# An order edge between each transfer of SyncE and ScalarE and the one written just before it

## The chip, the cores and the metric

The kernel runs on one core of one Trainium2 chip. The metric is the device time of one execution in microseconds (us); lower is better. The kernel before takes 667.28 us, the median of three runs (664.82 to 667.79). The engines are named as in the profile: PE (matmul), PEld (its weight loads), DVE (vector), ACT (scalar), POOL (GpSimd) and SP (sync). SP computes nothing: its queue only issues transfers. ACT both computes and issues transfers, and its queue is one list, in which a transfer that waits holds up the computation behind it.

## The reference

Two blocks run one after the other. The first is a delta-rule attention over 4 batches x 8 heads x 768 steps x 48 channels; the second is a feed-forward block on the 3072 tokens that come out of it.

```python
k_n = k / (np.linalg.norm(k, axis=-1, keepdims=True) + 1e-06)
for t in range(S):
    kt, vt, bt = (k_n[:, :, t], v[:, :, t], beta[:, :, t, None])
    y[:, :, t] = np.einsum('bhd,bhde->bhe', q[:, :, t], state)
    v_old = np.einsum('bhde,bhd->bhe', state, kt)
    state = state + bt[:, :, :, None] * np.einsum('bhd,bhe->bhde', kt, vt - v_old)
...
x = np.ascontiguousarray(attn_out.transpose(0, 2, 1, 3)).reshape(B * S, H * D)
h = x @ w_in            # 384 -> 2048
g = h * np.cos(h)
return (g @ w_out)      # 2048 -> 384
```

The two weight arrays come as 64-bit floats: the kernel loads them as pairs of 32-bit words and makes 32-bit floats of them itself.

## The kernel before

**Attention.** The 768 steps are cut into 24 units of 32 steps (`unit(n)`, n = 0 to 23), and two units make a pair m. For a unit, k, q and v are loaded (`load`, line 356; from unit 8 on q and k also as transposable blocks, `load_blocks`, line 375), a Gram matrix of the keys is made on PE (`gram`, line 611), scaled on DVE (line 622) and put into DRAM (`gram_put`, line 663). For each pair the Gram matrices are read back in another layout (`gram_get`, lines 676 and 684), and the triangular systems are inverted column by column (`invert`, lines 721 and 728): for the first pair on DVE, for the other eleven on POOL, which is the longest work of that engine. The inverse goes through DRAM (`put`, line 742) and comes back per unit as the tile `zt` (`get`, lines 753 and 761), which `solve` (line 851) needs. The state is carried from unit to unit on PE and DVE (`update`, line 876, `update_out`, line 884).

**Feed-forward.** Two units together give 256 tokens. Their hidden layer is made of products on PE, plain ones for the first two pairs of units (`hidden`, line 935), and a fast scheme with sums of blocks for the others (`layer`, line 1113, with copies of its banks on ACT, lines 1125 and 1127, and sums of x on POOL or DVE, line 1028). The gate h cos h goes through ACT, DVE, ACT, DVE (lines 976, 983, 992, 995), and the output layer through PE (lines 1136 and 1193), ACT or DVE (lines 1232 and 1245) and a store (line 1257). The weights come in 28 slices: `narrow_load` (line 473, tile `pairs`), `narrow_split` on ACT (lines 481 and 483), `narrow_shift` on DVE (lines 487 and 492), `narrow_add` on POOL (line 496).

**The order of the work** is written out by hand: `Order.LINE` is a list of all tasks, and `Order.run` emits them in this order. `Order.OTHER` says which transfers go on ACT's queue instead of SP's: 139 on ACT, 526 on SP. After the last task the loop at lines 1721 to 1725 gives every instruction an order edge to the one written before it on the same engine (`pin`, line 1697). Such an edge (`DependencyClass.NoSync`) is drawn when the program is built: it holds a place in the order, and it is no semaphore wait.

**What the build adds.** The build interleaves the five lists of instructions, hands out buffers of a pool as it goes, and gives every transfer of SP and ACT one of eight counters (DMAHW0 to DMAHW7) in turn, in the order in which it has placed the transfers of both queues. A transfer is issued only once the transfer before it on its counter has landed. In the built program nearly every transfer carries such a wait, for the transfer eight places earlier in that order, whichever queue that one is on. In this text this is the transfer's *predecessor*.

**Buffers.** The pool tag `g` has eight buffers (`GATES = 8`). The gate tiles `g_ffn`, the weight slices `pairs` and some small tiles take them in turn; whoever gets a buffer waits for the last user of that buffer.

Of the kernel before, what the change touches and what calls it, by code (L numbers as in the profile page):

```python
# [218 lines left out]
def kernel(  # L219
# [1477 lines left out]
    def pin(ins, on):  # L1697
        tc.add_manual_dep(
            ins,
            on.name,  # L1700
            mybir.DependencyInfo(
                mybir.DependencyClass.NoSync, mybir.DependencyReason.DATA
            ),
            reason="order",
        )
# [12 lines left out]
    order.run(wrote)  # L1718


    last = {}
    for ins in nc.cur_bb.bb.instructions:
        if ins.engine in last:
            pin(ins, last[ins.engine])
        last[ins.engine] = ins


# [29 lines left out]
```

## Time and profile before

| what | value |
|---|---|
| median of three runs | 667.28 us |
| lowest and highest | 664.82 and 667.79 us |
| span of the profiled execution | 663.5 us |
| PE busy | 595.1 us (90%) |
| POOL busy | 484.3 us (73%) |
| DVE busy | 504.2 us (76%) |
| ACT busy | 294.7 us (44%) |
| transfers on SP's queue (q1) | 160372 packets, 32.31 MB, 26.4% of 16 engines |
| transfers on ACT's queue (q10) | 54896 packets, 17.28 MB, 12.1% of 16 engines |
| mean granted TensorE clock | 0.952 |

The span runs from the first to the last instruction of one profiled execution. The profile gives no time of its own beside that span; the three timed runs lie 1.3 to 4.3 us above it. The profile's views are these: busy times by engine; 40 slices of the span; the chain of work that ended last; groups of instructions by line; waits, with who waited for whom; and the timeline of an engine. A row such as `ACT g_ffn L1125 <- DMA gb<-g_dr: 11.4, 1, 11.4` reads: the instruction of line 1125 on ACT started after 11.4 us of idle time, once, and what ended the wait was the landing of a transfer that writes `gb`.

### The profile page before, as it was taken

How to read it: one execution, taken by the hardware profiler on the slowest of the kernel's cores; microseconds unless marked ns; L12 is line 12 of the kernel's file. 1: busy time of each engine (PE TensorE's matmuls, PEld its weight loads, DVE VectorE, ACT ScalarE, POOL GpSimd, SP SyncE). 2: the span in 40 equal slices, each digit the busy share in tenths (PEclk: the TensorE clock that was granted, in tenths of full speed). 3: DMA queues.
4: the chain of work that ended last, by engine and by line, in shares of the span. 5: the costliest groups of instructions: out<-in, count | busy, mean ns of one | idle time of the engine just before them, and what ended most of it. 6: DMA issues, size and time to landing. Idle time of an engine off the chain costs nothing.

```text
span 663.5 us, 23460 instructions
## 1 busy us (share of the span) xinstructions
PE 595.1 (90%) x9784; PEld 559.0 (84%) x9784; DVE 504.2 (76%) x996; ACT 294.7 (44%) x518; POOL 484.3 (73%) x852
## 2 busy tenths in 40 slices
PE   3315799889999999999999999999789999999997
PEld 3304698677898999989999999999789999999996
DVE  5775588689799887868888888898758678667581
ACT  3424475454234544545545436444235453546340
POOL 4447888868898898888898988988666688413322
PEclk9855599989999999999999999999989999999999
DMA  8786764762164352344451462542311400200000
GB/s 173 166 185 155 180 139 120 156 133 43 44 113 62 64 94 43 74 85 71 67 100 27 80 98 41 95 78 52 73 24 33 92 10 26 34 2 26 1 24 25
DMA packets 215629, 51.52 MB, mean 78 GB/s; under 512 B 207076, under 2 KB 210420, under 8 KB 215524
## 3 DMA queue, kind: packets, MB, share of 16 engines
q1 hardware_dynamic: 160372, 32.31, 26.4%
q10 hardware_dynamic: 54896, 17.28, 12.1%
q8 instruction: 77, 1.26, 0.8%
q0 software_dynamic: 256, 0.45, 0.3%
q14 instruction: 28, 0.23, 0.1%
HBM read 39.24 MB, written 10.75 MB: 75 GB/s over the span
## 4 chain that ended last, share of the span: by engine, by line
PE 61%; POOL 19%; DMA 7%; DVE 4%; issue 4%; SPq 2%; ACT 1%; ACTq 0%; POOLq 0%; DVEq 0%
PE p_h L1113 20%; PE p_out L1193 20%; POOL z L728 8%; POOL part L721 7%; PE p_h L935 6%; PE p_out L1136 3%; DMA vp<-in_v_dram 3%; PE p_kq L781 2%; POOL x_sum L1028 2%; PE p_s L876 2%; PE p_kq L893 2%; PE p_u L851 2%; PE p_o L1193 2%; DMA pairs<-in_moe_w_in_dram 1%; PE p_g L611 1%
## 5 line engine op out<-in xcount | busy, mean ns | idle before, releaser
L721 POOL TENSOR_TENSOR part<-z,gb 128x126 f32<-128x126 f32 (+22 forms) x341 | 151.9, 445 | 36.2 <-ACT z L700 8.2
L728 POOL TENSOR_TENSOR z<-z,part 128x126 f32<-128x126 f32 (+22 forms) x341 | 155.3, 455 | 26.7
L1193 PE MATMUL p_out<-w_out,g_ffn 128*128 128x192 f32 x672 | 120.0, 329 | 0.0
L1193 PEld LDWEIGHTS p_out<-w_out,g_ffn 128*128 128x128 f32 x672 | 108.0, 190 | 1.2
L1209 POOL TENSOR_TENSOR g_ffn<-g_ffn 128x512 f32<-128x512 f32 x43 | 57.8, 1349 | 56.6 <-PE p_out L1193 30.9
L1113 PE MATMUL p_h<-x_sum,w_in 128*128 128x128 f32 x640 | 83.2, 279 | 7.9 <-ACT g_ffn L1125 6.4
L1193 PE MATMUL p_out<-w_sum,g_ffn 128*128 128x192 f32 x496 | 88.9, 328 | 0.1
L992 ACT ACTIVATE turns<-turns,halfpi 128x512 f32<-128x512 f32 x96 | 68.3, 719 | 42.5 <-DVE turns L983 35.6
L1113 PEld LDWEIGHTS p_h<-x_sum,w_in 128*128 128x128 f32 x640 | 78.4, 193 | 9.2 <-ACT g_ffn L1125 6.7
L1193 PEld LDWEIGHTS p_out<-w_sum,g_ffn 128*128 128x128 f32 x496 | 79.6, 190 | 0.7 <-DVE o L1245 0.3
L976 ACT ACTIVATE turns<-g_ffn,quarter_turn 128x512 int32<-128x512 f32 x70 | 50.1, 720 | 48.8 <-DVE g_ffn L1130 25.7
L1130 DVE TENSOR_TENSOR g_ffn<-g_ffn,p_h 128x512 f32<-128x512 f32 x80 | 54.6, 683 | 17.0 <-PE p_h L1113 14.9
L906 ACT COPY y<-p_kq 32x384 f32<-32x384 f32 x96 | 45.1, 470 | 37.2 <-PE p_kq L893 31.9
L995 DVE TENSOR_TENSOR g_ffn<-turns,g_ffn 128x512 f32<-128x512 f32 x70 | 53.3, 770 | 8.9 <-ACT turns L992 8.8
L983 DVE SCALAR_TENSOR_TENSOR turns<-g_ffn,turns 128x512 f32<-128x512 f32 x70 | 56.5, 812 | 1.6 <-ACT turns L976 1.4
L1113 PE MATMUL p_h<-x_sum,in_sum 128*128 128x128 f32 x400 | 53.8, 279 | 0.1
L935 PE MATMUL p_h<-x_ffn,w_in 128*128 128x128 f32 x384 | 48.8, 288 | 5.5 <-DVE g_ffn L995 5.5
L935 PEld LDWEIGHTS p_h<-x_ffn,w_in 128*128 128x128 f32 x384 | 46.9, 202 | 6.6 <-DVE g_ffn L995 5.9
L1113 PEld LDWEIGHTS p_h<-x_sum,in_sum 128*128 128x128 f32 x400 | 50.0, 194 | 0.9 <-ACT g_ffn L1125 0.4
L1245 DVE SCALAR_TENSOR_TENSOR o<-p_out,o 128x192 f32<-128x192 f32 x74 | 25.2, 353 | 31.5 <-PE p_out L1193 30.6
L530 POOL TENSOR_TENSOR knrm<-ksum,halves 128x16 f32<-128x16 f32 (+1 forms) x14 | 38.9, 2777 | 11.1 <-DVE ksum L518 11.0
L1113 PE MATMUL p_h<-x_ffn,w_in 128*128 128x128 f32 x320 | 43.1, 279 | 0.0
(133 smaller groups left out, 1011.0 us busy)
## 6 DMA issues: line engine op xcount, KB each, us to landing
pairs<-in_moe_w_out_dram SPq DMA_DIRECT2D x12, 384.0 KB
vp<-in_v_dram SPq DMA_DIRECT2D x88, 48.0 KB
pairs<-in_moe_w_in_dram ACTq DMA_DIRECT2D x7, 512.0 KB
gb<-g_dr ACTq DMA_DIRECT2D x12, 256.0 KB
kp<-in_k_dram SPq DMA_DIRECT2D x128, 24.0 KB
out_dram<-o ACTq DMA_DIRECT2D x14, 192.0 KB
pairs<-in_moe_w_in_dram SPq DMA_DIRECT2D x5, 512.0 KB
gb<-g_dr SPq DMA_DIRECT2D x10, 256.0 KB
```

The source lines that it names most:

```text
L721: eng.tensor_tensor(out=part, in0=z[:, 0:rows, j, None].to_broadcast(shape), in1=a[:, j, None, j + 1 :].to_broadcast(shape), op=ALU.mult,)
L728: eng.tensor_tensor(out=behind, in0=behind, in1=part, op=ALU.subtract)
L906: nc.scalar.copy(by_parity(y[quarter(b)]), p_kq[quarter(b ^ 1), :, b % 2])
L935: nc.tensor.matmul(p_h[:, i], w_in[:, t, (4 * k + i) * 128 : (4 * k + i + 1) * 128], xts[p][:, t, unit * 128 : (unit + 1) * 128], start=(i ...
L976: nc.scalar.activation(turns[p, f], hidden_of(p, f), AF.Identity, bias=quarter_turn, scale=TURN)
L983: nc.vector.scalar_tensor_tensor(out=r, in0=hidden_of(p, f), scalar=TURN, in1=t, op0=ALU.mult, op1=ALU.subtract,)
L992: nc.scalar.activation(r, r, AF.Sin, bias=halfpi, scale=2.0 * math.pi)
L995: nc.vector.tensor_tensor(out=place(p, f), in0=step_of(rests.pop((p, f)), f), in1=step_of(hidden_of(p, f), f), op=ALU.mult,)
L1113: nc.tensor.matmul(p_h[:, e], in_block(*w)[:, e], x_of(p, b), start=new and e == 0, stop=True, skip_group_check=True,)
L1130: nc.vector.tensor_tensor(out=part_of(p, to), in0=part_of(p, one), in1=part_of(p, two), op=op)
L1193: nc.tensor.matmul(p_o, left(p, part, a)[:, e % 4], right(e, b), start=(e == 0), stop=(e == FT // 2 - 1), skip_group_check=True,)
L1209: either(("left", p, x, s), nc.vector, nc.gpsimd).tensor_tensor(out=left(p, s, to), in0=left(p, s, one), in1=left(p, s, two), op=op)
```

## The change

The loop that pins each engine's instructions also remembers the last transfer that is not POOL's. If the next such transfer stands on the other queue, it gets an order edge to the one written before it. With the edges along each engine, all 665 transfers of SP and ACT then stand in one fixed order, that of `Order.LINE`. The edges are of the same kind as those already there. No instruction is added or taken away.

```diff
-    last = {}
+    last, before = {}, None
     for ins in nc.cur_bb.bb.instructions:
         if ins.engine in last:
             pin(ins, last[ins.engine])
         last[ins.engine] = ins
+        if isinstance(ins, mybir.InstDMACopy) and ins.engine != mybir.EngineType.Pool:
+            if before is not None and before.engine != ins.engine:
+                pin(ins, before)
+            before = ins
```

## The prediction

> **What bounds the kernel.** I read the page first, then the stretches, then the waits and timelines of the stretches where PE is not full. The first rows are the page's.
>
> ```profile
> span 663.5 us, 23460 instructions
> PE   3315799889999999999999999999789999999997
> POOL 4447888868898898888898988988666688413322
> DMA  8786764762164352344451462542311400200000
> PE 61%; POOL 19%; DMA 7%; DVE 4%; issue 4%; SPq 2%; ACT 1%; ACTq 0%; POOLq 0%; DVEq 0%
> ```
>
> One slice is 16.6 us. Counted from 1, PE is nearly full but for the first five slices, a dent in slices 8 and 9 (116 to 149 us), and one in slices 29 and 30 (464 to 498 us). The transfer engines are busy only at the start. POOL is at 8 to 9 tenths from slice 10 to slice 28, so what is late on POOL stays late there. The busy times by stretch (columns: stretch, length, PE, PEld, DVE, ACT, POOL, granted clock, transfer engines' share, GB/s) say the same:
>
> ```profile
> 0.00:66.00 66.00, 23.09 (x648) 19.38 (x648) 43.07 (x119) 24.66 (x45) 35.73 (x51) 0.72 0.79 170
> 126.00:150.00 24.00, 17.88 (x150) 16.34 (x143) 16.28 (x29) 11.12 (x21) 17.74 (x32) 0.93 0.72 144
> 470.00:484.00 14.00, 7.59 (x54) 7.30 (x53) 6.38 (x13) 2.57 (x6) 5.71 (x13) 0.86 0.49 91
> 484.00:664.00 180.00, 174.70 (x2298) 169.62 (x2298) 120.68 (x221) 75.91 (x130) 92.51 (x161) 0.98 0.12 26
> ```
>
> Behind 484 us PE is busy for 174.7 of 180 us and DMA for 0.12: a shift there goes to the end whole. Three places are open to transfers: the start, 126 to 150 us, and 470 to 484 us.
>
> **What the change does.** I compared the wait lists of the two built programs. The order on every queue is the same in both, and no wait between the two queues is added as such; what the edges fix is the order in which the eight counters are dealt. 387 of 665 transfers get another predecessor. In the program before, eight transfers wait for one that is written *after* them; in the program after none does. One pair of `g` buffers is exchanged as well. No instruction is added, so there is no issue time to price. The price of each edit is the landing of its new predecessor against the time at which the transfer was issued in this trace.
>
> **470 to 484 us: a wait goes (-6.7).** The timeline of ACT, then of SP:
>
> ```profile
> 470.16 0.32 ACTq L375 DMA_DIRECT2D qp<-in_k_dram  x1
> 470.57 0.59 ACT L1125 COPY p_h<-p_h 128x512 f32<-128x512 f32 x1
> 481.14 1.41 ACTq L375 DMA_DIRECT2D qp<-in_k_dram  x3
> 482.59 1.07 ACT L1125 COPY g_ffn<-p_h 128x512 f32<-128x512 f32 x2 [11.43 <-DMA gb<-g_dr]
> ```
> ```profile
> 476.67 0.37 SPq L742 DMA_DIRECT2D z_dr<-z  x1
> 477.27 1.35 SPq L684 DMA_DIRECT2D gb<-g_dr  x2
> ```
>
> ACT issues one of four block loads at 470.16, and the second only at 481.14. The second's predecessor is SP's `gb` load of 477.27, written four places after it, which stands behind SP's put of `z`, which waits for POOL's inverse. So ACT waits 10.7 us (481.14 - 470.48) for a transfer that it has no use for, and the two copies behind (line 1125) keep PE's banks occupied. The waits of 470 to 485 us give PE's price:
>
> ```profile
> ACT g_ffn L1125 <- DMA gb<-g_dr: 11.4, 1, 11.4
> PEld p_h L1113 <- ACT g_ffn L1125: 6.7, 1, 6.7
> ```
>
> After the change the three loads' predecessors are Gram puts that SP issued at 459.3 to 460.4 and that landed by 462.4, so ACT passes at once. Its copies are then done at about 476, and PE, which now stops at 477.0 and resumes at 483.72, goes on without a stop. What is late next there is SP's four `zt` loads, landed by 483.3; `solve` reads them at 493.39. With the shift of +1.9 below they land at 485.2, and PE, 4.8 early, comes at 488.5: 3.4 us to spare. POOL's next column (484.84) waits for the `gb` load at 481-482 as before and has some 4 us to spare. So I take the whole 6.7.
>
> **0 to 66 us: waits come (+4.7).** Here 32 transfers have a new predecessor that landed after their issue in this trace, 17 on SP (15.0 us in sum) and 15 on ACT (20.1 us). The chain of waits shows where landings carry the end (start, us, what):
>
> ```profile
> 24.55 6.13 DMA vp<-in_v_dram
> ...
> 44.66 3.92 DMA vp<-in_v_dram
> ...
> 61.88 4.14 DMA pairs<-in_moe_w_in_dram
> 66.03 2.75 DMA kp<-in_k_dram
> ```
>
> Written order makes SP's Gram put of 27.94 wait for the v load of 24.55, which lands at 30.68, and with the +0.5 carried from before it comes 3.25 late. ACT's Gram put of 37.94 then waits for a v load of 33.57 that landed at 39.67, itself 1.7 late: +3.5. ACT's `halves_z` loads (46.4 to 48.6) wait for the v load landed at 48.58: +4.5. SP's `halves_z` load of 53.29 waits for ACT's weight load landed at 54.97, itself +3.35: +5.1. The weight load of 61.88 and the k load of 66.03 come 4.7 late, and with them the squares on ACT (68.88), which PE waits for. A little is won too (a Gram step at 14.8 comes 1.2 earlier). Bounds: 0, because the transfer engines are busy 0.79 of this stretch and a transfer that is held leaves its share to those beside it, so that they land sooner; and 5.1, the largest delay on that path. I take 4.7, since every step of it is a landing in this trace.
>
> **126 to 150 us: 2.8 of these are given back.** The exchanged buffers: a gate tile (line 995) no longer takes the buffer of a weight slice that POOL still reads, and the weight load of SP at 129.38 takes it instead. The timelines of DVE and of PE:
>
> ```profile
> 132.27 0.69 DVE L995 TENSOR_TENSOR g_ffn<-turns,p_h 128x512 f32<-128x512 f32 x1 [5.41 <-POOL w_out L496]
> ```
> ```profile
> 133.02 2.94 PE L935 MATMUL p_h<-x_ffn,w_in 128*128 128x128 f32 x24 [2.81 <-DVE g_ffn L995]
> 138.66 4.57 PE L935 MATMUL p_h<-x_ffn,w_in 128*128 128x128 f32 x24 [2.70 <-DVE g_ffn L995]
> ```
>
> DVE's 5.41 us and PE's 2.81 + 2.70 fall away, which takes PE's +4.7 to about -0.4 at 143 us. But SP's load now waits for POOL's add (ends at 132.24 here, 137.3 with the +5.0 of that stretch, which is 4.7 and some 0.4 from a weight load on ACT at 116.19 whose new predecessor landed at 116.77), so it is 8.05 late, and what stands behind it on SP's queue (block loads, line 375; weight loads, line 473; v) is 4.4 late from 135.5 on. The weight slice issued at 138.66 lands 4.4 later, at 149.1; its split on ACT (145.99) comes 3.1 late, its shift on DVE (148.12) 1.9 late, then the key norms on POOL (151.88), and POOL carries +1.9 to the x sum of 187.34, for which PE waits at 188.16. So +1.9 is what stays of the start up to 477 us.
>
> **Sum:** +4.7 - 2.8 - 6.7 = -4.8. The profiled span of 663.5 becomes 658.7. The timed runs lie 1.3 to 4.3 above that span, the median 3.8; the change concerns nothing outside the span, so the median goes from 667.28 to **662.5**.
>
> **Rivals.**
>
> (a) *The start is cheaper.* If the start costs 0, the same path hands on -2.8 to 477 us, and the sum is -9.5: 657.8. For: the share of 0.79. Against: single landings of 6 us, not bandwidth, make that chain.
>
> (b) *The wait of 470 us has an heir.* If the `zt` loads or POOL's columns come 3.4 to 4 us later than the shift says, PE meets them, and about 4 of the 6.7 return: 666.5. For: SP's `zt` loads now have ACT's block loads as predecessors. Against: those would be issued at about 472.4, eight us ahead of them.
>
> (c) *Nothing moves.* The two queues use the same transfer engines, and if only the bytes count, the order between the queues is worth no more than the issue time, 0.3 to 0.5 us a transfer: 667.3. Against is the wait of 10.7 us above, which is no lack of bandwidth (share 0.49). [...]
>
> (d) *Slower: the two queues lock step in the first 66 us.* If SP's 17 waits add up, each landing later because the one before did, the start costs 15.0 in place of 4.7, and the sum is +5.5: 672.8. It makes the kernel slower from a start of 9.5 on. For: loads of 4 to 6 us each, in a chain that crosses from queue to queue. Against: by this trace the late ones overlap, and the path keeps 4.7.
>
> (e) *The edges don't do what their words say.* They are no waits on the chip: the built lists show none between the queues. If all 665 transfers really went one behind the other, 665 landings of at least 1.5 us would take about 1000 us. I give it no chance.
>
> **Chances.** Forecast 0.60, (a) 0.15, (b) 0.09, (c) 0.08, (d) 0.08. The likeliest is the forecast, 662.5. The range goes from 656.5 ((a) less 1.3 for the spread of the runs) to 667.5 ((b), (c) and the runs' own spread); it leaves out (d) and the thin ends, some 0.15. A measurement of this kernel can tell about 0.5% (3.3 us) from no change. Faster by more than that (below 663.9) are (a) and most of the forecast: 0.70; within it: 0.21; slower, (d) and an end of (c): 0.09.
>
> **What would show it.** In the profile after: no ACT wait on `gb` near 470 us, and slice 29 of PE a 9; DVE's 5.4 us on POOL's `w_out` gone, and SP's load of line 473 waiting for POOL instead; the squares of line 513 at 73 to 74 us instead of 68.9; the x sum near 189. Wrong would be the prediction if PE's wait at 477 us kept more than 3 us under another name, or if PE were more than 5 us late at 190 us.

## The result, and the profile after

The kernel takes 656.24 us with the edges (median of four runs, 655.82 to 659.10) and 666.77 us without them in the same comparison (the three runs told above and a fourth): a ratio of 0.9852, with a 95% interval of 0.9832 to 0.9873, or 10.5 us less (8.5 to 11.2). The forecast was 662.5 us, so the direction was right and the gain was a little more than twice the forecast 4.8. The profiled execution has a span of 657.3 us and a time of 659.1. This offset of 1.8 us is 1.7 to 1.9 in every run of this study for which both are known. One run of the kernel before, beside the first experiments, took 783.61 us at a mean granted clock of 0.776, where the others have 0.94 to 0.99; the ratios below leave it out.

The page of the kernel after, same rows as before:

```profile
span 657.3 us, 23467 instructions
PE   3306599989989999999999999999999999999996
POOL 4347888888889888888798998888858888413331
DMA  8796755664164334255451372354231410200000
PE 60%; POOL 20%; issue 3%; DMA 2%; DVE 1%; ACT 1%; SPq 0%; ACTq 0%; POOLq 0%
```

The dent of PE in slices 29 and 30 is gone, and slices 9 and 12 are at 8 tenths, where 8 and 9 were. DMA has fallen from 7% to 2% of the chain that ended last. The stretches (columns as before: stretch, length, PE, PEld, DVE, ACT, POOL, granted clock, transfer engines' share, GB/s):

```profile
0.00:66.00 66.00, 24.14 (x688) 20.00 (x692) 43.99 (x121) 24.93 (x45) 35.25 (x48) 1.00 0.79 169
126.00:150.00 24.00, 20.20 (x267) 17.98 (x266) 17.71 (x33) 12.36 (x23) 19.94 (x36) 1.00 0.74 151
470.00:484.00 14.00, 14.00 (x109) 14.00 (x108) 11.20 (x21) 4.80 (x9) 7.40 (x16) 1.00 0.49 94
484.00:657.00 173.00, 168.34 (x2260) 163.33 (x2258) 117.38 (x217) 74.55 (x127) 93.66 (x161) 1.00 0.13 27
```

From 470 to 484 us PE is busy for all 14.00 us, where it was busy for 7.59; the transfer engines' share there is 0.49 in both. In the first 66 us PE does no less than before (24.14 against 23.09 us).

**The place at 470 us.** The timeline of ACT in the kernel after, one row for each stretch of like instructions:

```profile
472.09 0.86 ACTq L375 DMA_DIRECT2D qp<-in_k_dram  x2
472.56 0.59 ACT L1125 COPY p_h<-p_h 128x512 f32<-128x512 f32 x1
472.99 1.04 ACTq L375 DMA_DIRECT2D qp<-in_k_dram  x2
474.95 0.59 ACT L1125 COPY g_ffn<-p_h 128x512 f32<-128x512 f32 x1 [1.80 <-DMA qp<-in_k_dram]
```

The four block loads leave within 2 us of each other (472.09 to 474.03), where the second waited for 10.7 us. The copy of line 1125, which came at 482.59, comes at 474.95. PE does not stop. Its timeline over the same work, first in the kernel after, then in the kernel before:

```profile
476.54 2.77 PE L1193 MATMUL p_out<-w_sum,g_ffn 128*128 128x192 f32 x16
479.14 1.05 PE L1113 MATMUL p_h<-x_sum,w_in 128*128 128x128 f32 x8
480.03 1.06 PE L1113 MATMUL p_h<-x_sum,in_sum 128*128 128x128 f32 x8
480.92 1.47 PE L1193 MATMUL p_out<-w_sum,g_ffn 128*128 128x192 f32 x8
...
487.19 0.68 PE L851 MATMUL p_u<-rhs,zt 64*64 64x48 f32 x32
```
```profile
474.55 2.77 PE L1193 MATMUL p_out<-w_sum,g_ffn 128*128 128x192 f32 x16
483.72 2.08 PE L1113 MATMUL p_h<-x_sum,w_in 128*128 128x128 f32 x8 [6.41 <-ACT g_ffn L1125]
485.59 1.70 PE L1113 MATMUL p_h<-x_sum,in_sum 128*128 128x128 f32 x8
487.12 1.47 PE L1193 MATMUL p_out<-w_sum,g_ffn 128*128 128x192 f32 x8
...
493.39 0.68 PE L851 MATMUL p_u<-rhs,zt 64*64 64x48 f32 x32
```

These two fences give two marks that all profiles of this study share. The *entry* is the start of the 16 matmuls of line 1193 ahead of the stop, the *exit* that of `solve` (line 851) behind it. From entry to exit the kernel before takes 493.39 - 474.55 = 18.84 us, the kernel after 487.19 - 476.54 = 10.65. That is 8.19 us, and not only the 6.57 by which the next matmuls begin sooner after the entry (483.72 - 474.55 = 9.17 against 2.60): the 16 matmuls of line 1113 behind the stop take 3.40 us (483.72 to 487.12), where the same take 1.78 without a stop (479.14 to 480.92). The columns of the stretches tell why; before, then after:

```profile
484.00:488.00 4.00, 4.00 (x22) 4.00 (x23) 1.37 (x3) 1.49 (x3) 2.45 (x10) 0.63 0.00 0
```
```profile
479.00:483.00 4.00, 4.00 (x33) 4.00 (x33) 2.57 (x5) 1.24 (x2) 0.00 (x0) 1.00 1.03 208
```

PE is busy for all of these 4 us in both, but it gets through 22 matmuls at a granted clock of 0.63 in the one and 33 at 1.00 in the other. The stretch in which the clock is down can be bounded: in the kernel before (first row) and in the run with early edges alone (second row, a kernel that has the stop too) it is 0.50 for 6.83 us.

```profile
480.10:486.93 6.83, 3.21 (x15) 3.21 (x16) 0.69 (x1) 2.89 (x5) 1.62 (x7) 0.50 0.43 67
```
```profile
480.55:487.38 6.83, 5.44 (x22) 5.45 (x23) 2.32 (x4) 2.89 (x5) 3.43 (x12) 0.50 0.15 18
```

It begins within the stop, so only its end falls on busy time of PE, 3.21 us in the one and 5.44 in the other. What the stage loses behind the stop is about half of that: 1.62 and 2.71 us. From the exit on both kernels take the same: 663.5 - 493.39 = 657.3 - 487.19 = 170.1 us (170.0 to 170.6 in all profiles of this study).

**The exchanged buffers at 130 us.** The waits of PE from 126 to 150 us, before and after, and the wait of SP's weight load after:

```profile
PE p_h L935 <- DVE g_ffn L995: 5.5, 2, 2.8
```
```profile
PE p_h L935 <- DVE g_ffn L995: 3.1, 1, 3.1
```
```profile
SPq L473 <- POOL w_out L496: 4.1, 1, 4.1
```

PE waits once instead of twice, 2.4 us less, and the load of line 473 waits for POOL's add instead. The wait of 3.1 us that is left has a new cause: DVE's gate of 145.87 us (line 995) stands behind POOL's `w_out` for 1.90 us. The x sum on POOL, at 187.34 us before, comes at 189.18, and PE waits for it:

```profile
189.69 1.16 PE L1113 MATMUL p_h<-x_sum,in_sum 128*128 128x128 f32 x8 [1.75 <-POOL x_sum L1028]
```

**The start.** The squares of line 513, at 68.88 us before, come at 70.11, not at 73 to 74:

```profile
70.11 0.84 ACT L513 ACTIVATE ksq<-kp 128x768 f32<-128x768 f32 x1 [4.78 <-DMA kp<-in_k_dram]
```

### The profile page after: what moved, and what is told of

It reads as the page before. It is cut to its first block, busy times and chain, and to the rows that moved or that the text cites. A ratio compares the mean times of both kernels' runs of the same rounds, so it can differ in the third digit from the quotient of the medians.

```text
span 657.3 us, 23467 instructions
## 1 busy us (share of the span) xinstructions
PE 593.9 (90%) x9784; PEld 557.6 (85%) x9784; DVE 501.9 (76%) x996; ACT 295.2 (45%) x518; POOL 486.6 (74%) x852
## 4 chain that ended last, share of the span: by engine, by line
PE 60%; POOL 20%; issue 3%; DMA 2%; DVE 1%; ACT 1%; SPq 0%; ACTq 0%; POOLq 0%
PE p_out L1193 22%; PE p_h L1113 22%; POOL part L721 8%; POOL z L728 8%; PE p_h L935 3%; PE p_kq L781 2%; PE p_s L876 2%; PE p_kq L893 2%; PE p_u L851 2%; PE p_o L1193 2%; POOL x_sum L1028 2%; PE p_g L611 1%; POOL g_ffn L1209 1%; DMA z_dr<-z 1%; PE p_z L914 1%
## 5 line engine op out<-in xcount | busy, mean ns | idle before, releaser
L721 POOL TENSOR_TENSOR part<-z,gb 128x126 f32<-128x126 f32 (+22 forms) x341 | 153.6, 450 | 34.5 <-DMA gb<-g_dr 8.5
L530 POOL TENSOR_TENSOR knrm<-ksum,halves 128x16 f32<-128x16 f32 (+1 forms) x14 | 37.3, 2665 | 9.7 <-DVE ksum L518 9.5
```

What stands on the lines that cost most here:

```text
L721: eng.tensor_tensor(out=part, in0=z[:, 0:rows, j, None].to_broadcast(shape), in1=a[:, j, None, j + 1 :].to_broadcast(shape), op=ALU.mult,)
```

## The experiments

All experiments are the kernel after with edges at some places only. `at` counts the transfers of SP and ACT in written order, 0 to 664; place 115 is issued at 68 us, places 268 to 271 at 193 us, place 590 at 448 us. Each is a line of this loop:

```diff
-    last, before = {}, None
+    last, before, at = {}, None, -1
...
+            at += 1
-            if before is not None and before.engine != ins.engine:
+            if before is not None and before.engine != ins.engine and CONDITION:
```

Theory A keeps the prediction's start: the early edges cost close to 5 us, so without them the kernel would be faster still. Theory B has the start near zero. The letters behind these are told in the expectations. Ratios are to the kernel before on the same chip, with 95% intervals.

| edges | median us | before | ratio | span | entry | exit | entry to exit |
|---|---|---|---|---|---|---|---|
| none (first profile) | 667.28 | | | 663.5 | 474.55 | 493.39 | 18.84 |
| none (before_1) | | | | 667.4 | 477.99 | 497.25 | 19.26 |
| none (before_2) | | | | 664.0 | 475.06 | 493.82 | 18.76 |
| none (before_3) | | | | 666.3 | 476.73 | 496.29 | 19.56 |
| early, below 115 | 665.00 | 667.65 | 0.9960 [0.9945, 0.9974] | 662.8 | 472.92 | 492.70 | 19.78 |
| middle, 115 to 269 | 666.08 | 667.65 | 0.9972 [0.9958, 0.9987] | 663.9 | 475.07 | 493.72 | 18.65 |
| all below 590 | 666.15 | 667.71 | 0.9979 [0.9961, 0.9998] | 664.0 | 474.93 | 493.83 | 18.90 |
| late, from 590 | 657.44 | 667.65 | 0.9854 [0.9838, 0.9870] | 655.6 | 474.83 | 485.49 | 10.66 |
| only 609 | 658.36 | 668.99 | 0.9834 [0.9817, 0.9850] | 657.0 | 476.24 | 486.89 | 10.65 |
| all from 115 | 657.99 | 667.65 | 0.9878 [0.9841, 0.9915] | 655.0 | 474.10 | 484.76 | 10.66 |
| early and late | 658.13 | 667.71 | 0.9863 [0.9840, 0.9886] | 656.2 | 474.97 | 485.62 | 10.65 |
| all (first profile) | 656.24 | 666.77 | 0.9852 [0.9832, 0.9873] | 657.3 | 476.54 | 487.19 | 10.65 |
| all (after_1) | 658.63 | 668.99 | 0.9827 [0.9797, 0.9856] | 657.0 | 476.08 | 486.73 | 10.65 |
| all (after_2) | 658.55, one run | 667.71 | | 656.8 | 475.85 | 486.50 | 10.65 |

The last column has two values and nothing between them: 18.65 to 19.78 us in the seven profiles without an edge at the late place, 10.65 or 10.66 in the seven with one.

**Early edges alone.**

```diff
+ CONDITION: at < 115
```

> The edges between the queues stand only among the first 115 transfers (about the first 66 us). Theory A (the start costs 4.7 us, as the profiled execution of before gave it): +4.7 us against before, some 671.4, since nothing gives it back. Theory B (the start costs about nothing on the mean; the profiled execution of before was a lucky one): 0 to +1.3 us, 666.8 to 668.1. With A the k load that the squares of line 513 wait for lands near 73.5 us, with B near 69 to 70 us.

665.0 us, 2.65 less than before (1.7 to 3.7). Theory A, which has the start cost time, falls, and the squares of line 513 come at 67.49 us, not near 73.5; Theory B expected no gain and misses it on this side. The late wait is there unchanged (PE's weight loads wait 6.6 us for ACT's copy).

**Middle edges alone.**

```diff
+ CONDITION: 115 <= at < 270
```

> The edges stand only among transfers 115 to 269 (about 66 to 195 us): the exchange of two g buffers, without the start and without the late wait. Theory A: -2.7 us (664.1), DVE's 5.4 us on POOL's w_out gone and the x sum of 187.3 earlier by 2.7. Theory B says the same of this part. Rival C (the exchange is worth nothing, since SP's held weight load takes the place of DVE's wait): within 0.7 us of before.

666.08 us, 1.6 less (0.9 to 2.8), so Rival C is out. The exchange of buffers happens: DVE's wait for POOL's `w_out` is gone from 120 to 150 us, PE's two waits become one of 3.1 us, and SP's load of line 473 waits 4.7 us for POOL. The x sum, expected 2.7 us earlier than 187.3, comes at 187.78; in the four profiles of the kernel before it comes at 187.3 to 191.2.

**Late edges alone.**

```diff
+ CONDITION: at >= 590
```

> The edges stand only from transfer 590 on (about 450 us): ACT's block loads no longer wait for SP's gb load, all else as before. Theory A, as predicted: -6.7 us (660.1), PE's stop at 477 gone. Theory D (the stop also costs a slow restart: the granted clock is 0.63 in 484 to 488 us of before and 1.00 in the same work of after): -8.1 us (658.7). Rival: an heir of the wait gives back 4 us, 664.

657.44 us, 10.2 less (8.7 to 10.8). In its profile the entry lies 0.3 us behind that of the first profile of before and the end 7.9 us ahead: 8.2 us by the marks, which are the stop and the slow matmuls behind it. Theory D, with 8.1, is right for the place. The median has some 2 us more, which the profile doesn't show.

**All but the early edges.**

```diff
+ CONDITION: at >= 115
```

> All edges but those among the first 115 transfers. Theory A: the start's 4.7 us are saved on top of the change, so some 651.5 us, faster than the changed kernel by 4.7. Theory B: the start is worth 0 to 1.3 us, so 655 to 656.5, the same as the changed kernel.

657.99 us, 9.7 less (5.7 to 10.6). Theory A's 651.5 is far outside. Taking the early edges away brings nothing.

**One edge.** Place 609 is SP's put of `z` (line 742), and the transfer written before it is ACT's last block load (line 375). The edge holds the put, and with it SP's `gb` load behind it, after the block loads in the order in which the counters are dealt.

```diff
+ CONDITION: at == 609
```

> One edge alone: SP's put of z (the transfer behind ACT's fourth block load in written order) stands behind that load, so the three block loads get older predecessors. If the wait of ACT at 470 us is the whole of the gain: the same as all edges from 590 on, -10.2 us (some 657.5). If other inversions of the order have a share in that gain: more than 1 us slower than 657.5.

658.36 us, a ratio of 0.9834 [0.9817, 0.9850], as good as with all edges on the same chip (658.63). A single edge of the order gives the whole gain. ACT's block loads leave at once, the last two (timeline of ACT) at 472.69 us, where the kernel before has them at 481.5 and 482.2:

```profile
472.69 1.04 ACTq L375 DMA_DIRECT2D qp<-in_k_dram  x2
```

**All but the late edges.**

```diff
+ CONDITION: at < 590
```

> All edges but those of the transfers from place 590 on, which are behind 460 us. The wait of 11.4 us on the gb load stays, and PE's stop of 6.4 to 6.8 us at 477 us with it. Theory B (the stop and the slow matmuls behind it are 8.1 us of the gain, the rest comes from the start and from the exchanged buffers): 2 to 4 us faster than the kernel before. Theory E (the late edge is the whole gain, and what the other edges showed alone is the spread of the start): within 1 us of the kernel before.

666.15 us, 1.6 less (0.1 to 2.6): between the two theories, and the interval reaches into both. The early and the middle edges together bring no more than either alone. The wait at 470 us is there as before, as ACT's timeline shows:

```profile
483.02 1.07 ACT L1125 COPY g_ffn<-p_h 128x512 f32<-128x512 f32 x2 [11.48 <-DMA gb<-g_dr]
```

**Early and late edges.** This joins the two parts that were the fastest alone.

```diff
+ CONDITION: at < 115 or at >= 590
```

> The edges of the first 115 transfers and of those from place 590 on, without those between, so that the two parts that were faster alone by 2.65 and 10.2 us stand together. Theory B, with the two adding up: 12 to 13 us faster than the kernel before, and some 2 us faster than all edges. Theory E: 10 to 11 us, the same as all edges.

658.13 us, 9.6 less (7.6 to 10.7). The gains don't add up, so no version here beats all edges.

**The same two kernels again**, for their profiles.

> The kernel before, unchanged, for another profile. Theory B (the first profiled execution was 2 us faster than the usual one): the span is 665 to 666 us, the stop of PE near 477 us is longer than 6.7 us or PE arrives there 1 to 2.5 us later. Theory A: the span is 663.5 and all is as in the first profile.

> As before_1, once more: whether the arrival of PE at 477 us or the length of its stop moves from execution to execution. Theory B: one of the two differs from the first profile by 1 to 2.5 us.

> The kernel before once more, for one further profile. Both theories: ACT waits 11.1 to 11.5 us on the gb load, PE stops for 6.4 to 6.8 us, and the granted clock is near 0.6 in the 4 us behind that stop. If executions differ by where the start leaves them, the squares of line 513 start at 69 to 72 us, and the span, 664 to 667.4 us, follows that difference.

> The changed kernel, unchanged, beside the others on one chip. If the late wait is all: 657.5, the same as one_edge. If the start and the exchange of buffers add to it: 654 to 655.5.

> The changed kernel once more, for one further profile. No stop of PE at 477 us and a granted clock of 1.00 behind it; squares of line 513 at 69 to 70.5 us, so no more than 1.5 us behind the first profile of before; span 654 to 657.5 us. A start that comes 4.7 us late in this profile would say that the prediction's chain of landings holds in some executions after all.

Four profiles of the kernel before span 663.5 to 667.4 us, and all four differ ahead of the entry (474.55 to 477.99) far more than behind it. This is no difference between chips alone: before_1 and before_2 ran on the same chip, 2.9 us apart at the entry. The first profile, on which the prediction is built, has the earliest entry, 1.5 us ahead of their mean of 476.1. The three of the kernel after have a mean of 476.2. Measured against the mean, the early and middle edges cost 0.1 us up to the entry; measured against the first profile, they cost 1.6.

Where the four part is seen on SP's queue: the Gram put of line 663, which the prediction has 3.25 us late by the edges. First profile of before, then before_1, then the kernel after:

```profile
27.94 0.38 SPq L663 DMA_DIRECT2D g_dr<-g  x1
```
```profile
30.67 0.38 SPq L663 DMA_DIRECT2D g_dr<-g  x1
```
```profile
30.60 0.38 SPq L663 DMA_DIRECT2D g_dr<-g  x1
```

Of the eight profiles without early edges, four issue this put at 27.2 to 27.9 us and four at 29.9 to 30.7, and their mean entries are 474.6 and 476.5. All six with early edges issue it at 29.8 to 30.6. So the edges do what the prediction says to this put, but half of the executions have that delay without them. In before_1 the squares come later than in any of the three profiles of the kernel after (71.48 us). In after_2 they come at 71.03, beyond the 70.5 that was expected.

Over all profiles the squares come at 69.4 us on average without early edges (8 profiles, 68.5 to 71.5) and at 69.3 with them (6 profiles, 67.5 to 71.0).

## Why the prediction was half right

**470 to 484 us, -6.7: right mechanism, size too small.** ACT's wait of 10.7 us for a transfer written after it was the cause of PE's stop, and the edge takes it away; that one edge alone gives the whole gain shows it. But the place is worth 8.2 us against the first profile and 19.1 - 10.65 = 8.5 us against the mean of the four profiles of before. The term priced only PE's idle time. It put the restart behind the stop at nothing, without a reason. Over the first 4 us from the restart the granted clock is 0.60 here and 0.50 to 0.65 in the six other profiles with the stop, and the 16 matmuls there lose 1.62 us. Over the seven profiles with the stop, what the stage takes beyond PE's later start is 1.4 to 2.7 us. The row for 484 to 664 us, which the prediction showed, hid this in a mean of 0.98. Why the clock falls there no run shows; measured is a clock of 0.50 for 6.83 us in two of the profiles, and a loss of 1.62 and 2.71 us behind the stop.

**0 to 66 us, +4.7: this step failed.** The forecast says "I take 4.7, since every step of it is a landing in this trace". Two things were wrong with it. First, the later links are far smaller than worked out. The put on SP is 2.7 us late (worked out: 3.25), ACT's Gram put 2.5 (3.5), but ACT's last `halves_z` load only 0.8 (4.5), SP's last one 1.6 (5.1) and the squares 1.2 (4.7). The chain breaks at the v load that was taken to land at 48.58 us at the earliest: in written order it is issued at 43.37 instead of 44.66, and it lands at 47.74. The landings are not fixed marks; the order that delays some transfers brings others forward. The lower bound of the term allowed for that, but by another cause: this load doesn't land sooner after its issue (4.37 us in place of 3.92), it is issued sooner. The relation that the bound rests on is there over the whole of the first profile of before, between loads of one kind: the 48 KB loads of line 356 on SP's queue land 4.0 us after their issue (median of 66) where the transfer engines are busy for more than 0.7 of that time, and 1.8 us (median of 6) where they are for less than 0.3; in the first profile of after it is 3.8 (55) and 1.8 (4). Second, the execution that was profiled is one of those in which the put isn't late without edges, and in half of them it is. Against the mean of eight profiles the squares come no later at all. Rival (a), a start that costs nothing, with 657.8 us, came closest. It is right on the start; its number is in part luck, since it hands on -2.8 to 477 us, where the means show +0.1, and prices the stop at 6.7.

**126 to 150 us, -2.8: the exchange is right, the match of the x sum is luck.** SP's load waits for POOL in DVE's place, as forecast. But PE's waits fall by 2.4 us and not by the 5.5 that were to go. The x sum comes at 189.18, as forecast ("near 189"), and not by the forecast's path: that had the start 4.7 us late and the key norms on POOL (line 530) 1.9 late, and they come 1.2 late and 0.16 early (151.72 against 151.88). POOL falls behind, by 2.0 us, only after them. Nor is the x sum late against more than the first profile: it comes at 188.9 on average in the four profiles of before and in the three of after. Alone, the middle edges are worth 1.6 us (0.9 to 2.8).

**Up to 477 us, +1.9.** Against the first profile the entry is 2.0 us later, close to the forecast, and the last leg of that path is there (PE's wait of 1.75 us for the x sum). This agreement is luck too, by the two paragraphs above. Against the mean of the four profiles of before it is 0.1. In the sum the start counts only by this +1.9, so what it cost the forecast is the 1.8 between the two.

**From span to time.** The forecast took the 3.8 us between the span of 663.5 and the median as something outside the span. The offset is 1.8; the other 2.0 us are that the profiled execution took less than the median. A step priced against it can't be added to the median as it was.

**The sum.** By the means of the profiled spans, the change takes 665.3 - 657.0 = 8.3 us: +0.1 up to the entry, -8.5 from entry to exit, and 0.1 behind. The forecast had +1.9 and -6.7 there, so the two terms missed 1.8 each. These are 3.5 of the 5.7 us by which the medians lie beyond the forecast; the rest is under what stays open.

**The other rivals.** (b), an heir of the wait: PE has no wait at 477 us, and `solve` reads `zt` at 487.19 without one. POOL waits 5.5 us for its `gb` load from 477 us on, but PE isn't waiting for that. (c), nothing moves: falls by 10.5 us; the single edge of place 609, which moves no byte, is worth 10.6. (d), lock step at the start: no profile with early edges has the squares more than 2.2 us behind the first profile of before.

**What stays open.** The medians differ by 9.2 to 10.5 us, the profiled spans by 8.3. Part of that is which executions were profiled. Beside the experiments 38 runs of the kernel before with a span on record have a mean of 666.1 us (663.3 to 668.5), and the first profile, with 663.5, is near their lower end; the nine runs of the kernel after have a mean of 655.6 (652.7 to 657.3), and its three profiles, with 657.0, lie 1.4 above it. With the late edges or the one edge alone the medians say 10.2 and 10.6, the marks 8.2 to 8.5. The early and middle edges bring 1.6 us together (0.1 to 2.6), but early alone 2.65, and nothing on top of the late ones that could be told from zero. The eight runs with the late edges or the one edge alone have a mean span of 656.1, so the remainder is there without the early and middle edges too. With 1 to 2 us it is smaller than what executions of one kernel differ by ahead of the entry, 3.4 us, and these runs don't assign it to a part. Why the put on SP has two positions was followed to a `gb` load that lands at 27.9 or at 30.6 us, and no further.

## What to carry to other kernels

When transfers of two queues share a set of completion counters, look in the built program for transfers that wait for one written later than themselves: each can be a place where one queue stands behind the other for nothing, and a single order edge there can be worth as much as ordering everything (here 658.36 and 658.63 us). Price a stop of PE with what comes behind it: read the granted clock of the first few us after it, not of the whole remainder (here 0.60 over 4 us, and 0.98 over 180). And profile the kernel before more than once before adding up shifts of a microsecond; a chain of landings from one execution is a sample, and its landings move when the order does.

## What the runs showed of the hardware

How the transfers stand behind each other can be read from the first profile of before. Each of the 665 transfers of SP and ACT raises one of eight semaphores, 83 or 84 of them each, and 597 carry a wait for the semaphore that they raise, in their own record or in a semaphore record just ahead of it on their queue. 657 have one ahead of them on their semaphore; 638 of these start behind all 16 landing marks of that one, and for the other 19 the profile has fewer than 16 marks between the two starts. There is one merged order of the two queues, and only one, in which the eight semaphores come in turn, and the same holds for the first profile of after. Between these two orders 387 transfers change the one that is eight places ahead. By the places in the order of after, eight transfers of the kernel before stand behind a later one, two of them among ACT's block loads at 481.14 and 482.15 us, and none of the kernel after does. Packets of SP's queue alone are up to 29 at once in the first profile of before, packets of ACT's queue alone up to 29, and those of both together up to 30.

The same load on SP (`gb`, line 676) was issued at 23.92 and at 24.42 us in two executions of the same kernel and landed at 27.88 and at 30.61: 4.0 and 6.2 us. The executions with the put behind it at 27.2 to 27.9 us and those with it at 29.9 to 30.7 are 1.9 us apart in the mean entry, which is half of the 3.9 us by which the spans of the kernel before differ (663.5 to 667.4). The clock doesn't explain that spread: the execution with the span of 667.4 us has a mean granted clock of 0.988, the one with 663.5 has 0.952. Where the granted clock did cost time is behind the stop at 477 us: it is 0.50 for 6.83 us, PE is busy for the last 3.21 us of these (5.44 with early edges alone), and the loss is about half of that. How much of the slow stretch falls on busy time differs from execution to execution, and with it the price of the same stop.
